# Attention and two MLPs on one core: the order of the attention steps, where its output is scaled, and one PSUM tile

## Chip, core and metric

The kernel runs on one core of one Trainium2 chip. Its engines are TensorE (PE in the profile), VectorE (DVE), ScalarE (ACT), GpSimd (POOL) and SyncE (SP), which issues most DMAs. The metric is device time in microseconds (us); a comparison uses the median of several runs.

## What is computed

```python
def _attn_ref(q, k, v):                       # 2 batches x 8 heads, 1152 keys, head width 64
    q_pool = q.reshape(B, H, S // 2, 2, D).mean(axis=3)          # 576 queries
    scores = q_pool @ k.T / sqrt(D)
    attn = exp(scores - max(scores))
    attn = attn / (sum(attn) + 1e-09)
    return attn @ v

x = attn_out.transpose(0, 2, 1, 3).reshape(1152, 512)            # one row per token
h = x @ w_in;  x = (h * tanh(softplus(h))) @ w_out               # Mish MLP, 512 -> 2048 -> 512
h = x @ w_in2; out = where(h > 0, h, exp(min(h, 0)) - 1) @ w_out2   # ELU MLP, same sizes
```

The MLP weights arrive as 64-bit floats and are converted on chip. Products that need the precision are made of three: each operand is split into a high part (`KH`, `QH`, `XH`, `wh`, `gh`) and the rest (`KL`, `QL`, `XL`, `wl`, `gl`).

## The kernel before

**Attention.** Two heads make a pair, and there are 8 pairs. A pair takes 18 steps: 9 tiles of 128 keys for its first 256 queries (chunk c=0), then 9 for the other 320 (c=1). An order written by hand fixes all work: `at(step, engine, f, ...)` puts a piece of work into a step, and a loop over the steps emits them. An offset below is the number of a step in its pair, 0 to 17. What the steps issue:

- `qk`: the transposed scores of one key tile, 8 matmuls into a tile S (L337, L339), then `exp` on ACT into `pt` (L345). The last two of the 8 subtract each query's maximum (row `top`).
- `peak_mm` and `peak`: to find those maxima, the scores of the next pair are computed once more in the other orientation (14 tiles M, L265 and L271), and DVE reduces each (L279). The list `WHEN` gives their steps relative to the pair's start. The maxima then travel through DRAM into a row: `top_out` (L314) and `top_in` (L320, L325, two or four small DMAs).
- `av`: the output before scaling, C = V times `pt`, two chunk accumulators (L432). It comes in bursts of two or three key tiles: bursts of c=0 at offsets 11, 13, 15 and 18 (the next pair's 0), of c=1 at 20, 22, 24 and 27.
- `add` on POOL (L358) and `total` on PE (tile T, L368) sum `pt` over the keys. The sum goes `spill` (ACT, L379), `sum_out` to DRAM (L385), `sum_in` (L389), `invert` on DVE (L411 adds 1e-9, L412 inverts), `inv_out` (L416), and `inv_in` as rows `rb` that fit C (L422).
- `scale` (DVE, L449) makes y = C times `rb` in SBUF; `token_high` (ACT, L454) and `token_low` (DVE, L459) split it into `XH` and `XL`, the MLP's input.
- SP also loads q, k and V (`load_v`, L232) of later pairs, and half a weight tile at a time (L107). The weights' conversion uses ACT, POOL and DVE (L117, L121, L126, L131, L132, L140, L143).

In PSUM, S, M, T and R (a transposed maximum, first pair only) share three slots of two banks in the order of issue: a tile can be written when the reader of the third tile before it has finished. C has two slots of one bank. In a step, `qk` and `exp` come first, then the M of that step, then `av`, then ACT's, DVE's, POOL's and SP's pieces. After the last step the loop goes on until all pieces are out; the last pair's sums are made wide (`total_wide`, `invert_wide`) without the way through DRAM.

**MLPs.** 96 units, each of 12 matmuls into a tile A (`h_mm`, L176), an activation, and 9 or 12 matmuls into accumulators B and C (`out_mm`, L668), three units later. They have PSUM pools of their own, taken when attention has given its pools back. The units of the first MLP take token blocks of 384 in the order 0, 1, 2, six units (of weight chunks) each at first; block 0 holds no token of the last pair.

Of the kernel before, what the change touches and what calls it, by code (L numbers as in the profile page):

```python
# [11 lines left out]
F32 = mybir.dt.float32  # L12
# [4 lines left out]
ALU = mybir.AluOpType  # L17
# [5 lines left out]
def tile_pool_attention_mish_elu_mlp(  # L23
# [40 lines left out]
    rawpool = ctx.enter_context(tc.tile_pool(name="rawpool", bufs=NR))  # L64
    dp = ctx.enter_context(tc.tile_pool(name="hop", bufs=2, space=bass.MemoryType.DRAM))
# [6 lines left out]
    wt, pools = {}, {}  # L72
# [73 lines left out]
    BANKS = {"A": 3, "B": 4, "C": 1}  # L146
    sums = cycle(("B", "B", "B", "B", "C"))

    def psum(tag):
        return pools["ps"].tile([P, 512], F32, tag=tag, name=tag, bufs=BANKS[tag])  # L150
# [30 lines left out]
    def attention():  # L181
        with ExitStack() as st:
            ap = st.enter_context(tc.tile_pool(name="attn", bufs=2))
            pools["f"] = st.enter_context(tc.tile_pool(name="f1", bufs=1))
            ps = st.enter_context(tc.tile_pool(name="pa", bufs=1, space=PSUM))
# [71 lines left out]
            def peak_mm(n, e):  # L257
# [4 lines left out]
                pt = sc[n, e] = ps.tile([P, 2, 512], F32, tag="S", name="M", bufs=3)  # L262
# [33 lines left out]
            def flip(t0, t1):  # L296
                pt = ps.tile([P, 2, 512], F32, tag="S", name="R", bufs=3)[:, 0]
# [32 lines left out]
            def qk(n, c, kt):  # L330
                o, w = cut[c][0], cut[c][1] - cut[c][0]
                pt = sc[n, c, kt] = ps.tile([P, 2, 512], F32, tag="S", name="S", bufs=3)
# [27 lines left out]
            def total(n, c):  # L360
                w = (cut[c][1] - cut[c][0]) // 2
                pt = sums_[n, c] = ps.tile([P, 2, 512], F32, tag="S", name="T", bufs=3)[:, 0]
# [24 lines left out]
            def sum_in(n, c):  # L387
                r = tots[n, c] = ap.tile([P, (cut[c][1] - cut[c][0]) // D], F32, tag=f"tot{c}", name="tot")
                nc.sync.dma_start(out=r, in_=hops.pop((n, c)))  # L389


            def total_wide(n, c):
                w = cut[c][1] - cut[c][0]
                pt = sums_[n, c] = ps.tile([P, 2, 512], F32, tag="S", name="T", bufs=3)[:, 0]
                p, a = pts[n, c], adds[n, c]
                srcs = [p[:, KT - 2], p[:, KT - 1], a[:, 0], a[:, 1]]
                for i, x in enumerate(srcs):
                    for h in range(2):
                        nc.tensor.matmul(
                            pt[half[h], :w], ones, x[:, h, :w], start=(i == 0), stop=(i == len(srcs) - 1)  # L400
                        )

            def invert_wide(n, c):
                w = cut[c][1] - cut[c][0]
# [406 lines left out]
```

## Time and profile before

| | |
|---|---|
| median of 3 runs | 674.32 us (673.21 to 674.74) |
| the profiled execution | 676.3 us, its span from first to last instruction 674.5 us |
| PE busy | 642.9 us, 95% of the span |
| DVE busy | 444.3 us, 66% |
| ACT busy | 341.9 us, 51% |
| POOL busy | 231.0 us, 34% |
| granted TensorE clock, mean | 0.989 of full speed |

Busy time of PE is overstated in attention: two matmuls that use different halves of the array run side by side, and a row's duration overlaps the next row's. What a matmul costs there is read from the distance between the starts of successive rows. The span splits in time into attention and the MLPs, so the stretches are to be read apart.

### The profile page before, as it was taken

What the parts mean: (1) busy time and instruction counts of PE and PEld (TensorE: products, weight loads), DVE (VectorE), ACT (ScalarE), POOL (GpSimd) and SP (SyncE); (2) the same over time, 40 slices, a digit from 0 to 9 for tenths busy, and PEclk for the clock granted to TensorE, in tenths of its full rate; (3) what the DMA queues carried; (4) which work ended last, traced back from release to release, by engine and by line L of the source; (5) the groups of instructions that cost most, each with busy time, mean ns of one, the idle gap of its engine ahead of it and who ended that gap; (6) DMA issues with size and microseconds to landing.
All of it is one profiled execution on the core that took longest, in us unless ns stands there. A gap on an engine that the chain in (4) does not pass through costs nothing.

```text
span 674.5 us, 11591 instructions
## 1 busy us (share of the span) xinstructions
PE 642.9 (95%) x4594; PEld 539.7 (80%) x4594; DVE 444.3 (66%) x700; ACT 341.9 (51%) x680; POOL 231.0 (34%) x216
## 2 busy tenths in 40 slices
PE   5998989898989899999999999999999999999997
PEld 3665656565656565999999999999999999999996
DVE  5756566566666635856645765776987788996543
ACT  2654545354545443643443545445666576665442
POOL 5877575756656543210110431333310011110000
PEclk9999999898989999999999999999999999999999
DMA  4323333333232113324123122222312321220111
GB/s 156 103 72 78 80 79 90 90 81 84 74 100 61 44 41 104 122 67 125 63 63 125 62 95 75 83 94 63 94 63 63 94 92 66 94 63 1 48 47 48
DMA packets 49615, 53.05 MB, mean 79 GB/s; under 512 B 16992, under 2 KB 38168, under 8 KB 49560
## 3 DMA queue, kind: packets, MB, share of 16 engines
q1 hardware_dynamic: 49048, 51.59, 25.9%
q8 instruction: 36, 0.59, 0.4%
q10 hardware_dynamic: 512, 0.72, 0.3%
q14 instruction: 19, 0.16, 0.1%
HBM read 49.84 MB, written 2.46 MB: 78 GB/s over the span
## 4 chain that ended last, share of the span: by engine, by line
PE 79%; DVE 10%; SPq 5%; DMA 4%; issue 1%; ACT 1%; DVEq 0%
PE A L176 30%; PE B L668 24%; PE S L337 6%; PE C L432 6%; PE C L668 6%; DVE stat L279 3%; SPq L325 2%; DMA rb<-pop 2%; PE M L265 2%; DVE XL L459 2%; PE T L368 2%; PE S L339 2%; DVE tot L411 1%; SPq L320 1%; PE M L271 1%
## 5 line engine op out<-in xcount | busy, mean ns | idle before, releaser
L345 ACT ACTIVATE pt<-S 128x512 f32<-128x512 f32 (+1 forms) x144 | 92.5, 651 | 95.6 <-PE S L339 57.0
L121 POOL TENSOR_SCALAR wf<-wf 128x512 f32<-128x512 f32 x64 | 42.8, 669 | 260.7 <-ACT wf L117 230.4
L279 DVE TENSOR_REDUCE stat<-M 128x2 f32<-128x768 f32 x96 | 89.8, 953 | 62.0 <-PE M L265 60.9
L176 PE MATMUL A<-XH,wh 128*128 128x384 f32 x384 | 128.9, 336 | 1.0 <-DVE y L449 1.0
L176 PE MATMUL A<-XH,wl 128*128 128x384 f32 x384 | 128.9, 336 | 0.0
L176 PE MATMUL A<-XL,wh 128*128 128x384 f32 x384 | 128.6, 335 | 0.0
L432 PE MATMUL C<-pt,vr 128*64 128x320 f32 (+1 forms) x576 | 85.7, 425 | 0.4 <-DVE y L449 0.4
L176 PEld LDWEIGHTS A<-XH,wh 128*128 128x128 f32 x384 | 72.1, 188 | 3.6 <-DVE y L449 1.6
L176 PEld LDWEIGHTS A<-XL,wh 128*128 128x128 f32 x384 | 72.1, 188 | 1.9
L358 POOL TENSOR_TENSOR add<-add,pt 128x512 f32<-128x512 f32 (+1 forms) x48 | 71.3, 1507 | 5.7 <-ACT pt L345 5.5
L358 POOL TENSOR_TENSOR add<-pt 128x512 f32<-128x512 f32 (+1 forms) x32 | 45.4, 1418 | 80.8 <-ACT pt L345 80.8
L176 PEld LDWEIGHTS A<-XH,wl 128*128 128x128 f32 x384 | 72.1, 188 | 0.0
L337 PE MATMUL S<-QH,KH 64*128 64x320 f32 (+1 forms) x288 | 53.8, 370 | 13.7 <-DVE stat L279 12.4
L337 PEld LDWEIGHTS S<-QH,KH 64*128 64x128 f32 x288 | 27.8, 189 | 46.1 <-DVE stat L279 20.2
L622 ACT ACTIVATE gh<-A 128x384 fp32r<-128x384 f32 x48 | 23.6, 492 | 78.9 <-PE A L176 78.9
L432 PEld LDWEIGHTS C<-pt,vr 128*64 128x64 f32 x576 | 36.4, 138 | 28.9 <-issue 9.7
L625 DVE TENSOR_TENSOR gl<-g,gh 128x384 fp32r<-128x384 f32 x48 | 32.0, 668 | 34.3 <-ACT g L623 34.2
L668 PE MATMUL B<-gh,wh 128*128 128x384 f32 x155 | 51.8, 334 | 0.0
L668 PE MATMUL B<-gl,wh 128*128 128x384 f32 x155 | 51.8, 334 | 0.0
L668 PE MATMUL B<-gh,wl 128*128 128x384 f32 x155 | 51.8, 334 | 0.0
L143 DVE TENSOR_TENSOR wl<-wf,wh 128x512 fp32r<-128x512 f32 x64 | 50.1, 783 | 0.7 <-ACT wh L140 0.7
L648 ACT CAST gh<-g 128x384 fp32r<-128x384 f32 x48 | 24.7, 514 | 48.1 <-DVE g L642 47.8
(103 smaller groups left out, 1330.5 us busy)
## 6 DMA issues: line engine op xcount, KB each, us to landing
raw<-in_moe_w_in_dram SPq DMA_DIRECT2D x28, 512.0 KB
raw<-in_moe_w_out_dram SPq DMA_DIRECT2D x28, 512.0 KB
vr<-in_v_dram SPq DMA_DIRECT2D x16, 288.0 KB
qr<-in_q_dram SPq DMA_DIRECT2D x14, 288.0 KB
kr<-in_k_dram SPq DMA_DIRECT2D x14, 288.0 KB
raw<-in_moe_w_in_dram SPq DMA_DIRECT2D x8, 256.0 KB
raw<-in_moe_w_out_dram SPq DMA_DIRECT2D x8, 256.0 KB
out_dram<-part SPq DMA_DIRECT2D x8, 256.0 KB
```

Of the source, the lines that this page charges most:

```text
L121: nc.gpsimd.tensor_scalar(self.f, self.f, HUGE, -HUGE, op0=ALU.min, op1=ALU.max)
L143: eng.tensor_tensor(self.l, self.f, self.h, op=ALU.subtract)
L176: nc.tensor.matmul(pt[:, :TB], w[:, kk * P:(kk + 1) * P], x[:, kk, tk], start=(i == 0), stop=(i == len(terms) - 1))
L279: nc.vector.tensor_reduce(m[:, t, :, j], pt[:, :, :KB], axis=AX.X, op=ALU.max)
L337: nc.tensor.matmul(pt[:, h, :w], x[half[h], kk], y[half[h], cols], start=(i == 0), stop=False)
L345: nc.scalar.activation(pts[n, c][:, kt], sc.pop((n, c, kt))[:, :, :w], AF.Exp, scale=SCALE)
L358: nc.gpsimd.tensor_tensor(d, d if i is None else p[:, i], p[:, j], op=ALU.add)
L432: nc.tensor.matmul(acc[n, c][half[h], :w], vs[n][:, h, kt, :], pts[n, c][:, kt, h, :], start=(kt == 0), stop=(kt == KT - 1),)
L622: nc.scalar.activation(gh, h, AF.Mish)
L625: nc.vector.tensor_tensor(gl, g, gh, op=ALU.subtract)
L648: nc.scalar.copy(gh, g)
L668: nc.tensor.matmul(pt, l, r, start=(first and i == 0), stop=(final and i == 2))
```

## The change

- The bursts of `av` have two key tiles and stand in every second step, at even offsets 10 to 26.
- In odd steps the M of the step is issued ahead of `qk`, in even steps behind it. `WHEN` changes; the last M of a pair comes one step earlier.
- `total` comes at offsets 12 and 20 (before 15 and 24), and the pieces behind it move with it; the last pair is no exception any more. `spill` adds the 1e-9 while it copies, so `invert` is one instruction. V is loaded at offsets 2 and 6 (before 9 of the pair ahead, and 2).
- `scale` works in place, in PSUM; `token_high` and `token_low` read it there. A list "rest" of DVE pieces comes behind the reduction of the step.
- One tile `banks` holds all 8 PSUM banks: 0 to 5 are the ring of attention's tiles, 6 and 7 the two accumulators; the MLPs use 0 to 2 for A and 3 to 7 in turn for the rest.
- The step loop ends 9 steps after the last `qk`. What is left of the last pair (`inv_in`, `scale`, `token_high`, `token_low` of c=1) is emitted in MLP units 0 to 2. Three weight tiles of the MLPs are read in the last pair already.

The diff, cut to its core (the removed functions `total_wide` and `invert_wide` and repeated replacements of a pool's tile by `take()` are left out):

```diff
+    banks = const_ps.tile([P, 8, 512], F32, name="banks")
+    turns = {"A": cycle(range(3)), "B": cycle(range(3, 8))}
     def psum(tag):
-        return pools["ps"].tile([P, 512], F32, tag=tag, name=tag, bufs=BANKS[tag])
+        return banks[:, next(turns[tag])]
...
+            ring = cycle(range(3))
+            def take():
+                i = 2 * next(ring)
+                return banks[:, i:i + 2]
...
-                nc.scalar.copy(r[:, :w], sums_.pop((n, c))[:, :w])
+                nc.scalar.activation(r[:, :w], sums_.pop((n, c))[:, :w], AF.Copy, bias=1e-9)
...
             def invert(n, c):
                 r = tots[n, c]
-                nc.vector.tensor_scalar(r, r, 1e-9, None, op0=ALU.add)
                 nc.vector.reciprocal(r, r)
...
-                    acc[n, c] = ps.tile([P, 512], F32, tag="C", name="C", bufs=2)
+                    acc[n, c] = banks[:, 6 + c]
...
-                x = xs[n, c] = ap.tile([P, w], F32, tag=f"y{c}", name="y", bufs=1)
-                nc.vector.tensor_tensor(x, acc.pop((n, c))[:, :w], rbs.pop((n, c)), op=ALU.mult)
+                x = xs[n, c] = acc.pop((n, c))[:, :w]
+                nc.vector.tensor_tensor(x, x, rbs.pop((n, c)), op=ALU.mult)
...
-            WHEN = [-13, -11, -10, -9, -8, -7, -6, -5, -4, -2, -1, 0, 1, 2]
+            WHEN = [-13, -12, -11, -10, -9, -8, -7, -5, -4, -3, -2, -1, 0, 1]
...
-                        at(s0 - 9 + 11 * i, "sp", load_v, n, i)
+                        at(s0 + [2, 6][i], "sp", load_v, n, i)
...
-                        at(u0 + KT + [2, 2, 4, 4, 6, 6, 9, 9, 9][kt], "av", av, n, c, kt)
-                    t0 = u0 + KT + 6
-                    if n < n_pairs - 1:
-                        at(t0 + 2, "sp", sum_out, n, c)
-                        at(t0 + 4, "sp", sum_in, n, c)
-                        at(t0 + 7, "dve", invert, n, c)
-                        at(t0 + 8, "sp", inv_out, n, c)
-                        at(t0 + 10, "sp", inv_in, n, c)
-                        at(t0 + 12, "dve", scale, n, c)
...
+                        at(s0 + 10 + (kt + 9 * c) // 2 * 2, "av", av, n, c, kt)
+                    t0 = s0 + 12 + 8 * c
+                    at(t0, "av", total, n, c)
+                    at(t0 + 1, "pre", spill, n, c)
+                    at(t0 + 1, "sp", sum_out, n, c)
+                    at(t0 + 3, "sp", sum_in, n, c)
+                    at(t0 + 5, "rest", invert, n, c)
+                    at(t0 + 5, "sp", inv_out, n, c)
+                    at(t0 + 7, "sp", inv_in, n, c)
+                    at(t0 + 10, "rest", scale, n, c)
+                    at(t0 + 11, "act", token_high, n, c)
+                    at(t0 + 12, "rest", token_low, n, c)
+            for r, x, y in (7, NW, 0), (11, NW, 1), (22, NW + 1, 0):
+                at(last - NS + r, "sp", early, x, y)
...
-            while s < last or todo or going:
+            while s < last + 9:
...
+                if s % 2:
+                    for f in by["peak"]:
+                        f()
                 if s < last:
                     qk(n, c, kt)
                     exp(n, c, kt)
-                for f in by["peak"]:
-                    f()
+                if s % 2 == 0:
+                    for f in by["peak"]:
+                        f()
...
+            for x, e in sorted(todo):
+                after.setdefault((x - s) // 2, []).extend(todo[x, e])
```

Three places show what the order becomes. On TensorE, in the middle of a pair (offsets around 11 of a later pair), before: S is L337 and L339, M is L265, the burst is L432.

```order
L265 MATMUL M<-KH,QH 128x384 x2
L337 MATMUL S<-QH,KH 128x320 x2
L337 MATMUL S<-QH,KL 128x320 x2
L337 MATMUL S<-QL,KH 128x320 x2
L339 MATMUL S<-top_81,unit 128x320 x2
L265 MATMUL M<-KH,QH 128x384 x2
L432 MATMUL C<-pt,vr 64x256 x4
L337 MATMUL S<-QH,KH 128x320 x2
L337 MATMUL S<-QH,KL 128x320 x2
L337 MATMUL S<-QL,KH 128x320 x2
L339 MATMUL S<-top_81,unit 128x320 x2
L265 MATMUL M<-KH,QH 128x384 x2
```

The same place of the changed kernel, where every tile is a part of `banks`: S is L344 and L346, M is L272, the burst L420.

```order
L272 MATMUL banks<-KH,QH 128x384 x2
L420 MATMUL banks<-pt,vr 64x256 x4
L272 MATMUL banks<-KH,QH 128x384 x2
L344 MATMUL banks<-QH,KH 128x320 x2
L344 MATMUL banks<-QH,KL 128x320 x2
L344 MATMUL banks<-QL,KH 128x320 x2
L346 MATMUL banks<-top_85,unit 128x320 x2
L344 MATMUL banks<-QH,KH 128x320 x2
L344 MATMUL banks<-QH,KL 128x320 x2
L344 MATMUL banks<-QL,KH 128x320 x2
L346 MATMUL banks<-top_85,unit 128x320 x2
L272 MATMUL banks<-KH,QH 128x384 x2
```

S and M alternated; now the two M of two steps stand around the burst and the two S behind them.

On VectorE, the stretch of a pair in which c=1 of the pair before is inverted; before (L459 is `token_low`, L411 and L412 `invert`, L449 `scale`):

```order
L459 TENSOR_TENSOR XL<-y,XH 128x256
L411 TENSOR_SCALAR tot<-tot 128x5
L412 RECIPROCAL tot<-tot 128x5
L279 TENSOR_REDUCE stat<-M 128x2 x4
L449 TENSOR_TENSOR y<-C,rb 128x320
L279 TENSOR_REDUCE stat<-M 128x2
```

And of the changed kernel (L447 `token_low`, L400 `invert`, L437 `scale`, L286 and L298 the reductions):

```order
L447 TENSOR_TENSOR XL<-banks,XH 128x256
L286 TENSOR_REDUCE stat<-banks 128x2
L400 RECIPROCAL tot<-tot 128x5
L286 TENSOR_REDUCE stat<-banks 128x2 x3
L298 TENSOR_REDUCE neg<-stat 128x4
L286 TENSOR_REDUCE stat<-banks 128x2
L437 TENSOR_TENSOR banks<-banks,rb 128x320
```

The adding instruction is gone, and a reduction stands between `token_low` and `invert`.

On SP's queue, where a pair begins, before (L416 `inv_out`, L320 and L325 `top_in`, L422 `inv_in`, L385 `sum_out`):

```order
L416 DMA pop<-tot 128x4
L320 DMA top_81<-hopm 1x256x1
L325 DMA top_81<-hopm 1x64x1
L320 DMA top_81<-hopm 1x256x1
L325 DMA top_81<-hopm 1x64x1
L107 DMA raw<-in_moe_w_out_dram 128x512
L422 DMA rb<-pop 64x256 x2
L385 DMA hop<-sum 4x160
L232 DMA vr<-in_v_dram 128x576
L389 DMA tot<-hop 128x5
```

And of the changed kernel (L392 `sum_out`, L327 and L332 `top_in`, L396 `sum_in`, L239 `load_v`, L404 `inv_out`, L410 `inv_in`):

```order
L392 DMA hop<-sum 4x160
L327 DMA top_85<-hopm 1x256x1
L332 DMA top_85<-hopm 1x64x1
L327 DMA top_85<-hopm 1x256x1
L332 DMA top_85<-hopm 1x64x1
L396 DMA tot<-hop 128x5
L239 DMA vr<-in_v_dram 128x576
L404 DMA pop<-tot 128x5
L109 DMA raw<-in_moe_w_out_dram 128x512
L410 DMA rb<-pop 64x320 x2
```

The four DMAs of `top_in` stood between `inv_out` and `inv_in`; now they stand between `sum_out` and `sum_in`, with the second half of V behind them.

## Rows read from the trace of the kernel before

**Rows 1.** Windows: us, then busy time of each engine, clock, DMA.

```profile
core 0: us, PE busy (x) PEld busy (x) DVE busy (x) ACT busy (x) POOL busy (x), PEclk, DMA share, GB/s
39.26:232.10 192.84, 177.21 (x1845) 115.69 (x1843) 123.32 (x177) 96.03 (x179) 123.57 (x90) 0.96 0.31 78
71.46:102.61 31.15, 28.43 (x311) 18.67 (x309) 20.65 (x30) 16.08 (x31) 20.66 (x15) 1.00 0.32 80
102.61:135.87 33.26, 30.25 (x309) 19.78 (x307) 20.73 (x30) 16.07 (x31) 20.63 (x15) 0.95 0.34 86
232.10:269.51 37.41, 34.95 (x335) 21.52 (x333) 17.81 (x33) 15.00 (x30) 14.97 (x11) 1.00 0.26 75
269.51:674.50 404.99, 400.69 (x2160) 381.62 (x2160) 280.02 (x460) 211.58 (x437) 64.47 (x80) 1.00 0.24 75
```

**Rows 2.** Timeline of PE: start, duration, what, idle before it and its releaser.

```profile
95.39 0.34 PE L265 MATMUL M<-KH,QH 64*128 64x384 f32 x2
97.72 0.41 PE L337 MATMUL S<-QH,KH 64*128 64x320 f32 x2 [1.99 <-DVE stat L279]
```

**Rows 3.** Timeline of DVE in the same stretch, and at 119.90.

```profile
93.60 1.57 DVE L459 TENSOR_TENSOR XL<-y,XH 128x256 fp32r<-128x256 f32 x1
95.09 1.51 DVE L411 TENSOR_SCALAR tot<-tot 128x5 f32<-128x5 f32 x1
...
96.74 1.78 DVE L279 TENSOR_REDUCE stat<-M 128x2 f32<-128x768 f32 x2
...
119.90 0.42 DVE L449 TENSOR_TENSOR y<-C,rb 128x256 f32<-128x256 f32 x1 [1.77 <-DMA rb<-pop]
```

**Rows 4.** Timeline of POOL at the same times.

```profile
93.33 1.55 POOL L358 TENSOR_TENSOR add<-pt 128x640 f32<-128x640 f32 x1 [1.95 <-ACT pt L345]
94.84 3.22 POOL L358 TENSOR_TENSOR add<-add,pt 128x640 f32<-128x640 f32 x2
...
117.36 2.77 POOL L252 TENSOR_TENSOR KL<-kr,KH 128x576 fp32r<-128x576 f32 x2
```

**Rows 5.** Timeline of PE, two stretches that show the distances between starts.

```profile
90.64 1.08 PE L432 MATMUL C<-pt,vr 128*64 128x256 f32 x8
91.66 0.42 PE L337 MATMUL S<-QH,KH 64*128 64x320 f32 x2
...
92.34 0.34 PE L265 MATMUL M<-KH,QH 64*128 64x384 f32 x2
...
111.48 0.39 PE L337 MATMUL S<-QH,KH 64*128 64x256 f32 x2
...
112.05 0.34 PE L265 MATMUL M<-KH,QH 64*128 64x384 f32 x2
...
112.80 1.30 PE L432 MATMUL C<-pt,vr 128*64 128x320 f32 x8
114.03 0.75 PE L368 MATMUL T<-pt,ones 128*32 128x160 f32 x16
...
115.25 0.39 PE L337 MATMUL S<-QH,KH 64*128 64x256 f32 x2
```

**Rows 6.** Timeline of SP's queue: start and duration of each issue.

```profile
104.96 0.43 SPq L232 DMA_DIRECT2D vr<-in_v_dram  x1
...
111.27 0.67 SPq L320 DMA_DIRECT2D top<-hopm  x1
...
115.06 0.88 SPq L325 DMA_DIRECT2D top<-hopm  x1
...
116.61 1.14 SPq L422 DMA_DIRECT2D rb<-pop  x2
...
252.59 0.33 SPq L416 DMA_DIRECT2D pop<-tot  x1
254.04 1.11 SPq L422 DMA_DIRECT2D rb<-pop  x2
```

**Rows 7.** Windows, one microsecond behind the load of V.

```profile
108.00:109.00 1.00, 1.00 (x8) 0.35 (x8) 1.00 (x4) 1.00 (x4) 0.11 (x1) 1.00 0.00 0
```

More of the change, by code (lines that the diff above doesn't have):

```diff
@@ L64, in tile_pool_attention_mish_elu_mlp @@
     rawpool = ctx.enter_context(tc.tile_pool(name="rawpool", bufs=NR))
+    const_ps = ctx.enter_context(tc.tile_pool(name="psum", bufs=1, space=PSUM))
+    late = ctx.enter_context(tc.tile_pool(name="late", bufs=1))
     dp = ctx.enter_context(tc.tile_pool(name="hop", bufs=2, space=bass.MemoryType.DRAM))
@@ L261, in peak_mm @@
                     neg[n] = ap.tile([P, NQ + 1, 2], F32R, tag="neg", name="neg")
-                pt = sc[n, e] = ps.tile([P, 2, 512], F32, tag="S", name="M", bufs=3)
+                pt = sc[n, e] = take()
                 if t < NQ:
@@ L296, in flip @@
             def flip(t0, t1):
-                pt = ps.tile([P, 2, 512], F32, tag="S", name="R", bufs=3)[:, 0]
+                pt = take()[:, 0]
                 for t in range(t0, t1):
@@ L387, in sum_in @@
             def sum_in(n, c):
-                r = tots[n, c] = ap.tile([P, (cut[c][1] - cut[c][0]) // D], F32, tag=f"tot{c}", name="tot")
+                r = tots[n, c] = late.tile([P, (cut[c][1] - cut[c][0]) // D], F32, tag=f"tot{c}", name="tot")
                 nc.sync.dma_start(out=r, in_=hops.pop((n, c)))
[L392 to L404, printed above, removed]
-                rb = rbs[n, c] = ap.tile([P, w], F32, tag=f"rb{c}", name="rb")
-                nc.vector.tensor_scalar(rb, sums_.pop((n, c))[:, :w], 1e-9, None, op0=ALU.add)
-                nc.vector.reciprocal(rb, rb)
             def invert(n, c):
                 r = tots[n, c]
-                nc.vector.tensor_scalar(r, r, 1e-9, None, op0=ALU.add)
                 nc.vector.reciprocal(r, r)
@@ L419, in inv_in @@
                 hop = hops.pop((n, c))
-                rb = rbs[n, c] = ap.tile([P, cut[c][1] - cut[c][0]], F32, tag=f"rb{c}", name="rb")
+                rb = rbs[n, c] = late.tile([P, cut[c][1] - cut[c][0]], F32, tag=f"rb{c}", name="rb")
                 for h in range(2):
@@ L579, in attention @@
                 s += 1
-            assert not pieces
+            assert not pieces and not going
+            for x, e in sorted(todo):
+                after.setdefault((x - s) // 2, []).extend(todo[x, e])
     def mlps():
@@ L657, in out_mm @@
                     if first:
-                        acc[m] = psum(next(sums))
+                        acc[m] = psum("B")
                     if layer == 0:
@@ L757, in mlps @@
                 go(u)
+                for f in after.pop(u, []):
+                    f()
                 between()
@@ L764, in mlps @@
                     when.pop(0)
-                    g = Weights(x, y)
+                    g = ahead.pop(0) if ahead else Weights(x, y)
                     assert u + 5 <= first_use[x] + AHEAD * y, (x, y, u)
                     going.append(g)
-                    g.read()
+                    if not hasattr(g, "moves"):
+                        g.read()
                     break
-            assert not loads and not going and not later
+            assert not loads and not going and not later and not after
     with tc.manual_schedule():
```

37 lines of the change are left out of this document (13 added, 24 removed).

## The prediction

> **What bounds the kernel now.** I read the windows first, cut where a pair's first S starts. The MLPs (269.51 to the end) keep PE busy for 400.69 of 404.99 us at full clock; the change leaves their matmuls as they are, so nothing is to be had there. Attention is another matter: six pairs, 39.26 to 232.10, take 192.84 us, 32.14 each, and no engine is full: of a pair of 31.15 us, DVE has 20.65, POOL 20.66, ACT 16.08 [rows 1].
>
> To see what PE itself needs, I took distances between starts [rows 5]. A burst of two key tiles takes 1.02 us for c=0 (90.64 to 91.66) and 1.23 for c=1 (112.80 to 114.03); an S beside a burst 0.68 for c=1 and 0.57 for c=0 (91.66 to 92.34, 111.48 to 112.05); an M with such an S 0.75, so M is 0.18; T of c=1 1.22, and by its columns about 1.0 for c=0 (an estimate). The three wide matmuls of the last two M run one after another, about 0.3 each (an estimate from M's columns). A pair: S 9 x (0.57 + 0.68) = 11.25; twelve M 2.2; wide M 0.9; C 4.5 x (1.02 + 1.23) = 10.1; T 2.2. That is 26.6 us. So **a pair waits 5.5 us**.
>
> Where, the timelines side by side show. The largest single wait is in every pair: PE stands 1.99 us before the S at 97.72 for DVE's reduction [rows 2]. DVE is late because `token_low` took 1.57 us and the adding instruction of `invert` 1.51, on 256 and 5 elements a partition; they end when POOL's additions end (93.33 + 1.55 = 94.88; 94.84 with two of 1.6) [rows 3, 4]. The scaling at 119.90, which reads C in PSUM and only one operand in SBUF, took 0.42 while POOL worked from 117.36 to 120.13 [rows 3, 4]. The rest of the waiting is spread: DVE itself waits for `rb` (1.77 us at 119.90), which SP could ask for only after `top_in`'s four DMAs, 111.27 to 115.94 [rows 3, 6], and with S and M alternating, an S reuses the slot of the M before last, so it waits whenever DVE is late.
>
> **The change, part by part.**
>
> *`invert` in one instruction, `token_low` from PSUM.* The adding instruction goes (1.51 us in this pair; `spill` adds while it copies, at the price of a copy). `token_low` now has one SBUF operand like the scaling, so I take 0.42 for it instead of 1.57; the bound above is 1.57, if it still waits for POOL. DVE's two late microseconds go, and with them the 1.99 us wait. The scaling in place writes PSUM rather than SBUF; no row shows that, I take the same 0.42, and up to 0.8 as a bound; it stands at M-free steps (offsets 4 and 12), where no reduction is behind it, so that bound too is covered.
>
> *The order of a pair of steps.* S M, burst, M S instead of S M S M with a burst somewhere. In the ring of three the M behind the burst needs the S of the step before, the S need the S and M before the burst: all are read during the burst. The one tight place is the M of the next even step, which needs the reduction of the odd M: 0.4 for M to land (0.34 long at 95.39, rather more behind a burst), 0.9 for the reduction (1.78 for two), 0.1 to hand over, together 1.4; PE reaches it after M and two S, 1.32 in c=0 and 1.54 in c=1 [rows 2, 3, 5]. With five such places I count 0.5 us a pair. `token_low` of c=1 stands before such a reduction: 0.3. Two steps cost 0.57 x 2 + 0.18 x 2 + 1.23 = 2.73, DVE's two reductions 1.8: 0.9 us of DVE are free in every two steps, and the weights' pieces lie at offsets without M.
>
> *The way of the sums through SP.* `top_in`'s block of 4.7 us has left the way from `invert` to `scale` and entered the one from `total` to `invert` for c=1. From T's end: copy 0.5 (estimate), `sum_out` 0.5 (estimate from the other issues), block 4.7, `sum_in` with its landing 1.8 (1.45 from an issue's start to the next DMA that needs it, 252.59 to 254.04): 7.5 us [rows 6]. On PE the steps between are 0.6 + 2.5 + 2.7 and then the reduction, 0.9 and its hand-over: 6.8. `invert` is 0.7 late; behind it stand the reductions of offsets 8 and 9, but DVE's free 0.9 takes most of it. I take 0.3, bounds 0 and 2. Then `inv_out` and its landing 1.45, `inv_in` 1.14, landing 2.15 (117.75 to 119.90) and a weight load's issue in between: 5.3 to `rb`, 13.0 after T [rows 3, 6], and `scale` is reached at 12.8. It is covered by T at offset 12, which has no M.
>
> *V's second half* stands behind `sum_in` on SP: issued about 6.1 us after T's end. The load of 104.96 had landed by 108.00, where nothing moves any more: 3.0 us [rows 6, 7]. So it lands at 9.2, and its first burst (offset 10) starts at 10.3: 0.6 + 2.5 + 2.7 + 2.9 + S and M 0.9, and 0.7 of waits. Nothing, with 1.1 to spare.
>
> *One PSUM tile; last pair; early weight reads.* An accumulator's bank is now held until `token_low` has read it (offsets 6 and 14); the next burst into it comes at 10 and 18: nothing. Any MLP wait by the common tile I take as nothing, up to 1 us at the start. The last pair and its tail are 37.41 us [rows 1]; after: S 11.25, wide M 0.9, C 5.5 + 4.6 + 5.5, T 1.2 + 1.0 + 1.2, 31.2, and 1.0 of waits: 32.2. It saves 5.2, bounds 3.5 and 6.2. c=1's scaling lies in MLP units 0 to 2; its tokens are first read in unit 12, 12 units of 4 us off.
>
> *The sum.* Waits of a pair 0.5 + 0.3 + 0.3, and 0.3 for small ones: 1.4, so 28.0 us (bounds 27.1 with half a microsecond of waits and 30.3). Six pairs save 6 x 4.1 = 24.8; the last 5.2; the first pair, where PE waits for loads and DVE, 0 (1.5 either way); the MLPs 0. Together 30.0. The profiled execution has 676.3 us (span 674.5), 2.0 above the median of 674.32; so 646.3 there, and **644.3** as a median.
>
> **A clock that goes on falling** is the first rival. The granted clock was 0.95 over 102.61 to 135.87 and 1.00 over 71.46 to 102.61 (33.26 against 31.15 us), 0.96 over six pairs: parts of them ran at 1.2 instead of 2.4 GHz, after PE had stood in the 1.99 us wait [rows 1, 2]. My 28.0 has it at 1.00. If it stays at 0.96 with the many short waits of a ring, six pairs of 28 lose 0.04 x 168 = 6.7 us: 651. Against it: the pair at 1.00 has short waits too, and the long one goes. The Trainium skill's page "TensorE: Matmul & The Clock Gate", section "A second HAM failure mode: psum-queue depth-cycling", says that short stops between matmul groups that cycle through PSUM slots can make the clock go up and down; by that rule this rival would hold, and the trace agrees only in so far as losing pairs exist.
>
> **Other rivals.** *SP's queue is the new bound*: `sum_in` or V comes 2 us later than I count, since `top_in`'s issues vary, and steps are shorter, so that fewer microseconds lie between the same number of steps. Then DVE or PE waits 2 us more in every pair, 30.0: 656. For it speaks that DVE waits for `rb` today already. *It doesn't do what it says*: the reductions' wait comes back in other places, as PE's order only moves it, and the pair stays above 31.5: 668 to 674, the last pair's gain alone remaining. Against it: DVE has 10 us free in a pair and loses 3 us of work. *Slower*: V's second half. If its landing came 6.5 us later than I count, the burst at offset 10 would stand 5.4 us in seven pairs, 38 us against 30 saved: 682. It decides against the change from 5.4 us late on (30 / 7 + 1.1), which asks for SP to be held by a wait that I have not seen.
>
> **How the numbers follow.** My forecast (a pair of 27.1 to 29.2) 0.55: 644.3, by itself 636 to 652. SP's queue 0.20, the clock 0.08, no effect on the pairs 0.09, slower 0.08. 636 is the sum with all lower bounds (6 x 5.0 + 6.2 + 1.5 = 38), 661 with all upper ones (6 x 1.8 + 3.5 - 1.5 = 13); the range 635 to 661 takes in the first three cases, and leaves out 0.17. A change of 0.2%, 1.3 us, is about what a measurement of this kernel can tell from none: faster 0.88, same 0.04, slower 0.08.
>
> **What would show it.** Right: windows from one pair's first S to the next of about 28 us, six alike, at clock 1.00; no PE wait of 2 us; `token_low` near 0.42 whatever POOL does; MLP matmuls starting near 239 with the same 405 behind them. Wrong: PE's bursts waiting for a DMA at offset 10 (V), DVE waiting long for `tot` or `rb` with PE's S or M behind it, a clock under 0.98 in the pairs, or pairs at 30 us and more.

## Result and the profile after

The changed kernel takes **652.38 us** (median of 4 runs, 651.91 to 652.93) against 674.48 us for the kernel before in the same call (673.21 to 674.74): a ratio of 0.9676, 95% interval 0.9659 to 0.9693. 644.3 was predicted, with a range of 635 to 661. One execution among all the runs below, at a granted clock of 0.85 from its first stretch to its last (709.5 us), is left out of the medians. Line numbers below are those of the changed kernel unless "before" is said.

Its windows, cut where a pair's first S starts (us; then busy time of each engine; granted clock, DMA share, GB/s), answer to [rows 1]:

```profile
core 0: us, PE busy (x) PEld busy (x) DVE busy (x) ACT busy (x) POOL busy (x), PEclk, DMA share, GB/s
13.69:40.94 27.25, 24.97 (x249) 18.23 (x251) 16.90 (x22) 14.14 (x27) 19.81 (x15) 1.00 0.33 94
40.94:212.28 171.34, 167.34 (x1846) 111.92 (x1844) 112.88 (x169) 91.19 (x180) 121.33 (x90) 1.00 0.39 88
98.31:126.62 28.31, 27.86 (x311) 18.65 (x309) 18.62 (x29) 15.20 (x30) 20.04 (x16) 1.00 0.41 98
212.28:244.34 32.06, 31.99 (x359) 20.18 (x355) 10.65 (x21) 15.47 (x29) 15.40 (x12) 1.00 0.33 85
244.34:650.10 405.76, 401.33 (x2162) 383.36 (x2160) 280.48 (x465) 211.76 (x438) 64.90 (x80) 1.00 0.24 77
```

Six pairs take 171.34 us, 28.56 each, instead of 192.84, and the clock is 1.00 in all. Set beside the terms of the prediction, in the two profiled executions (676.3 and 651.91 us):

| | predicted | measured |
|---|---|---|
| up to the first S | 0 | -0.68 (14.37 to 13.69) |
| first pair | 0 | **+2.36** (24.89 to 27.25) |
| six pairs | -24.8 | **-21.5** |
| last pair and tail | -5.2 | -5.35 (37.41 to 32.06) |
| MLPs | 0 | +0.77 |
| sum | -30.0 | -24.4 |

Where the 1.99 us wait stood [rows 2], nothing of that size is left: the longest wait that the profile lists for PE in the six pairs is 0.43 us. In the timeline of all engines of the changed kernel at offsets 6 and 7, `token_low` (L447) takes 0.41 us while POOL adds from 51.37 to 53.89, instead of 1.57 [rows 3], and the reduction behind it follows the M:

```profile
51.37 2.52 POOL L365 TENSOR_TENSOR add<-add,pt 128x512 f32<-128x512 f32 x2
52.68 0.41 DVE L447 TENSOR_TENSOR XL<-banks,XH 128x256 fp32r<-128x256 f32 x1
52.93 0.44 PE L272 MATMUL banks<-KH,QH 64*128 64x384 f32 x2
53.41 0.96 DVE L286 TENSOR_REDUCE stat<-banks 128x2 f32<-128x768 f32 x1 [0.31 <-PE banks L272]
```

What is left of PE's waiting stands where an even step's M needs the reduction of the odd step's M. The timeline of all engines at offset 6:

```profile
107.59 0.96 DVE L286 TENSOR_REDUCE stat<-banks 128x2 f32<-128x768 f32 x1 [1.32 <-ACT wh L142]
107.99 0.60 ACT L352 ACTIVATE pt<-banks 128x512 f32<-128x512 f32 x1 [0.39 <-PE banks L346]
108.14 0.28 PE L346 MATMUL banks<-top,unit 64*128 64x256 f32 x2
108.70 0.44 PE L272 MATMUL banks<-KH,QH 64*128 64x384 f32 x2 [0.28 <-ACT pt L352]
109.07 1.30 PE L420 MATMUL banks<-pt,vr 128*64 128x320 f32 x8
```

The profile puts this wait down to the exponential of step 5's S, which ends 0.04 us behind the reduction (108.59 and 108.55). By the ring the M takes the slot that the reduction reads, and in the run with short reductions, below, the same M starts while that exponential still runs; so it is the reduction that it waits for.

### The profile page after: what moved, and what is told of

Its sections match the earlier page's. It is cut to its first block, busy times and chain, and to the rows that moved or that the text cites. A ratio compares the mean times of both kernels' runs of the same rounds, so it can differ in the third digit from the quotient of the medians.

```text
span 650.1 us, 11772 instructions
## 1 busy us (share of the span) xinstructions
PE 631.7 (97%) x4626; PEld 536.9 (83%) x4626; DVE 428.2 (66%) x684; ACT 336.5 (52%) x682; POOL 229.0 (35%) x216
## 4 chain that ended last, share of the span: by engine, by line
PE 87%; DVE 4%; DMA 4%; SPq 1%; ACT 1%; issue 1%; POOL 0%; DVEq 0%; ACTq 0%
PE banks L178 31%; PE banks L661 30%; PE banks L420 10%; PE banks L344 6%; PE banks L272 4%; DVE stat L286 3%; PE banks L375 2%; PE banks L346 2%; DMA pop<-tot 1%; DMA rb<-pop 1%; PE banks L278 1%; DMA hopm<-neg 1%; DMA tot<-hop 1%; ACT pt L352 1%; DMA qr<-in_q_dram 1%
## 5 line engine op out<-in xcount | busy, mean ns | idle before, releaser
L352 ACT ACTIVATE pt<-banks 128x512 f32<-128x512 f32 (+1 forms) x144 | 88.8, 651 | 85.0 <-PE banks L346 75.2
L178 PE MATMUL banks<-XH,wh 128*128 128x384 f32 x384 | 129.5, 337 | 0.0
L178 PE MATMUL banks<-XL,wh 128*128 128x384 f32 x384 | 129.4, 337 | 0.0
L178 PE MATMUL banks<-XH,wl 128*128 128x384 f32 x384 | 129.4, 337 | 0.0
L286 DVE TENSOR_REDUCE stat<-banks 128x2 f32<-128x768 f32 x96 | 91.0, 957 | 49.8 <-PE banks L272 39.1
L420 PE MATMUL banks<-pt,vr 128*64 128x320 f32 (+1 forms) x576 | 85.5, 418 | 0.0
L178 PEld LDWEIGHTS banks<-XH,wh 128*128 128x128 f32 x384 | 72.0, 188 | 2.3 <-issue 0.5
L178 PEld LDWEIGHTS banks<-XL,wh 128*128 128x128 f32 x384 | 72.0, 188 | 1.8
L178 PEld LDWEIGHTS banks<-XH,wl 128*128 128x128 f32 x384 | 72.0, 188 | 0.0
L661 PE MATMUL banks<-gh,wl 128*128 128x384 f32 x192 | 64.5, 336 | 0.0
L420 PEld LDWEIGHTS banks<-pt,vr 128*64 128x64 f32 x576 | 35.3, 136 | 27.5 <-issue 10.5
L272 PE MATMUL banks<-KH,QH 64*128 64x384 f32 x192 | 43.2, 455 | 11.8 <-ACT KH L256 6.3
```

Of the source, the lines that this page charges most:

```text
L178: nc.tensor.matmul(pt[:, :TB], w[:, kk * P:(kk + 1) * P], x[:, kk, tk], start=(i == 0), stop=(i == len(terms) - 1))
L272: nc.tensor.matmul(pt[:, h, :KB], qh[n][half[h], t * P:(t + 1) * P], kh[n][half[h], j * KB:(j + 1) * KB], start=True, stop=True,)
L286: nc.vector.tensor_reduce(m[:, t, :, j], pt[:, :, :KB], axis=AX.X, op=ALU.max)
L352: nc.scalar.activation(pts[n, c][:, kt], sc.pop((n, c, kt))[:, :, :w], AF.Exp, scale=SCALE)
L420: nc.tensor.matmul(acc[n, c][half[h], :w], vs[n][:, h, kt, :], pts[n, c][:, kt, h, :], start=(kt == 0), stop=(kt == KT - 1),)
L661: nc.tensor.matmul(pt, l, r, start=(first and i == 0), stop=(final and i == 2))
```

## Experiments

All pair lengths are distances between the first S of successive pairs in the profiled execution, as above; medians are set beside the kernel before as it ran in the same call (674.5 to 677.9).

**The kernel before, profiled again.** No edit.

> The kernel before, unchanged, profiled a second time. Theory: the 2.0 us by which its profiled execution lay above the median came from stretches at a lower clock (0.95 and 0.96 in some pairs), and other executions lose less: the pairs that were long then (33.26, 32.93) are not the same ones here, several are near 31.2, and six pairs take 189 to 191 us instead of 192.8, with a total of 673 to 675. Rival: the clock falls in the same pairs in every execution, six pairs 192.5 to 193, and the 2.0 us have another place.

675.86 us. Six pairs, 39.30 to 231.74, take 192.44 us. Two of its windows:

```profile
102.96:136.12 33.16, 29.99 (x309) 19.63 (x307) 20.71 (x30) 16.04 (x31) 20.60 (x15) 0.95 0.34 87
136.12:167.27 31.15, 28.75 (x309) 18.76 (x308) 20.64 (x30) 16.07 (x31) 20.60 (x15) 1.00 0.32 80
```

Both expectations miss. The clock falls in partly other pairs than in the first profile, but the total of the six is nearly the same: three of them are at 0.95 here, four were there. A pair at full clock takes 31.12 to 31.55 us in the two executions, one at 0.95 takes 32.2 to 33.3; set against the full-clock pairs of the same execution, that is 1.0 us a pair on average over the six in the first, and 0.7 here.

**VectorE's relief alone, in the old order.**

```diff
-  nc.scalar.copy(r[:, :w], sums_.pop((n, c))[:, :w])
+  nc.scalar.activation(r[:, :w], sums_.pop((n, c))[:, :w], AF.Copy, bias=1e-9)
-  nc.vector.tensor_scalar(r, r, 1e-9, None, op0=ALU.add)          # invert
-  x = xs[n, c] = ap.tile([P, w], F32, tag=f"y{c}", name="y", bufs=1)
-  nc.vector.tensor_tensor(x, acc.pop((n, c))[:, :w], rbs.pop((n, c)), op=ALU.mult)
+  x = xs[n, c] = acc.pop((n, c))[:, :w]
+  nc.vector.tensor_tensor(x, x, rbs.pop((n, c)), op=ALU.mult)
-  at(t0 + 14, "act", token_high, n, c);  at(t0 + 16, "dve", token_low, n, c)
+  at(t0 + 13, "act", token_high, n, c);  at(t0 + 13, "rest", token_low, n, c)
```

> The kernel before with VectorE's relief alone: the 1e-9 goes into the copy, the scaling works in place in PSUM, the bursts and the order of S and M stay; token_high and token_low come earlier (offset 10 of the next pair for c=0, 1 for c=1), behind the reduction, since PSUM's accumulator is held until then. Theory (the 1.99 us wait of PE was VectorE waiting for POOL's additions): that wait goes in every pair, about 2.0 us each, and with it the fall of the clock, up to 1 us: pairs of 29 to 30.2, 655 to 662 in all. Rival (the reductions come late for another reason, the order of S and M with uneven bursts): pairs stay above 31, 668 to 674.

664.84 us (median of three executions, 664.15 to 667.16), ratio 0.983 (0.9785 to 0.9875). The pairs are read from another profile of the same kernel:

> The same kernel as e2_before_relief, profiled once more, since that profile has the clock at 0.85 from the first to the last stretch, the MLPs too, and its pairs can't be read. Theory A (with the 1.99 us wait gone, the old order needs what the changed kernel without alternation needs, 28.6 us): pairs at clock 1.00 take 28.6 to 29.2, some are longer at a lower clock, total 661 to 667. Theory B (other waits take its place): pairs at clock 1.00 stay at 30 to 30.8, with PE waits over 0.5 us listed.

667.56 us. Five of six pairs take 28.76 to 29.96 us, one 34.57. PE's waits in one pair, and at the start of the MLPs (line numbers of that kernel):

```profile
107.01 1.30 PE L431 MATMUL C<-pt,vr 128*64 128x320 f32 x8 [0.52 <-DVE XL L458]
...
260.83 0.41 PE L176 MATMUL A<-XH,wh 128*128 128x384 f32 x1 [2.24 <-DVE XL L458]
```

The 1.99 us wait is gone in all six pairs. Five of them come down from 31.15 to 29.4 on average, between the two theories: bursts now wait 0.3 to 0.6 us for an accumulator that is held until `token_low`. In the sixth, at a clock of 0.90, an M waits 1.86 us (87.96) for a reduction ahead of which VectorE's `scale` had stood 3.18 us for `rb` (86.61). In the tail, which still has its old form, that holding costs 3.3 us (40.75 instead of 37.41), which hides about a third of the pairs' gain in the total and puts it above the 655 to 662 that were expected.

**The relief taken back, in the new order.** The same edit the other way round, in the changed kernel.

> The changed kernel with VectorE's relief taken back: the adding instruction stands ahead of the reciprocal again, and the scaling writes SBUF, so token_low has two SBUF operands. Theory (contention with POOL is half of the gain, whatever the order): token_low at offset 6 and the adding instruction at offset 7 again last until POOL's additions end, about 1.5 us later for the reductions behind them, and PE waits 1.5 to 2.5 us more in every pair: 30.2 to 31 a pair, 662 to 668 in all. Rival (the even bursts alone give VectorE enough room): pairs under 29.2, 656 or less.

665.6 us (664.72 to 666.16), ratio 0.9832 (0.9797 to 0.9867): 13 us above the changed kernel. Pairs of 30.68 to 31.22. The two longest of PE's waits in one:

```profile
85.68 0.44 PE L272 MATMUL banks<-KH,QH 64*128 64x384 f32 x2 [0.78 <-DVE stat L286]
99.98 0.44 PE L272 MATMUL banks<-KH,QH 64*128 64x384 f32 x2 [1.26 <-DVE stat L286]
```

As the theory had it: with alternation, each slow `token_low` (1.48 at 83.27, 1.98 for two at 97.07) stands before a tight reduction.

**No alternation: M behind S in every step.**

```diff
-  if s % 2:            # "peak" ahead of qk
+  if 0:
-  if s % 2 == 0:       # "peak" behind exp
+  if 1:
```

> The changed kernel with M behind S in every step, odd ones too. Theory (the alternation is worth little: with a burst in every second step a slot's reader always has a burst's time): pairs 28.2 to 29.0, 650 to 655 in all; the wait of the first pair at its seventh step goes as well, up to 1 us. Rival (the alternation is what removes the waits): pairs of 30 and more, 662 or more in all.

651.37 us (650.31 to 652.59), ratio 0.9625 (0.9583 to 0.9668): not slower than the changed kernel. Six pairs take 171.79 us, 28.63 each. The alternation is worth nothing here; "little" was expected. PE has small waits of another kind in this order:

```profile
109.96 0.28 PE L346 MATMUL banks<-top,unit 64*128 64x256 f32 x2
110.29 0.44 PE L272 MATMUL banks<-KH,QH 64*128 64x384 f32 x2
```

The M takes the slot of the S before last, whose exponential (the first of two, 1.25 us together from 109.64) ends only then: 0.33 us after the last matmuls of S instead of 0.12 (106.28 to 106.40), five times a pair, and the burst behind such an M comes 0.1 later as well.

**Neither alternation nor relief.** Both edits; what remains of the change are the bursts in every second step, the earlier sums with their pieces in other steps, and the tail; further V's loads, `WHEN`, and the steps of the weights' conversion, which the change moves too (the core of the diff doesn't show it). No run takes any of these back by itself, but for the places of the two pieces of VectorE below.

> The changed kernel with M behind S in every step and VectorE's relief taken back, so that the bursts in every second step with the earlier sums and the new tail remain. Theory (bursts and relief are each worth something by themselves): pairs of 29.5 to 31, 657 to 667. Rival A (the even bursts alone are the gain): under 29, 655 or less. Rival B (they are nothing without the relief): 31.5 and more, 668 to 671.

652.33 us (651.06 to 657.6), ratio 0.9661 (0.9618 to 0.9704). My theory falls, rival A nearly holds: four pairs of 28.63 to 28.65, the others 29.64 and 30.05. `token_low` is as slow as ever, in a pair in which PE waits nowhere over 0.15 us; the adding instruction takes 0.51 there:

```profile
107.84 1.51 DVE L448 TENSOR_TENSOR XL<-y,XH 128x256 fp32r<-128x256 f32 x1
109.28 0.95 DVE L286 TENSOR_REDUCE stat<-banks 128x2 f32<-128x768 f32 x1
110.14 0.51 DVE L400 TENSOR_SCALAR tot<-tot 128x5 f32<-128x5 f32 x1
```

In the two longer pairs PE waits 1.06 us (141.78) and 1.34 us (212.10) for reductions that stand behind a slow piece and a late DMA: the sum, for which VectorE waits 0.89 us ahead of an adding instruction of 0.91 (139.74), and `rb`, for which it waits 2.05 us at 205.18, with two `token_low` of 3.25 us behind it (207.92). So without the relief a late sum or `rb` still reaches PE. What differs from [rows 3] in the other four is that a reduction stands between `token_low` and the adding instruction. That asked for two more runs, the same idea from both sides.

**The kernel before, with the two pieces in different steps.**

```diff
-  at(t0 + 14, "act", token_high, n, c);  at(t0 + 16, "dve", token_low, n, c)
+  at(t0 + 13, "act", token_high, n, c);  at(t0 + 14, "dve", token_low, n, c)
```

> The kernel before with one edit: token_low stands two steps earlier (offset 11 of the next pair for c=0, 2 for c=1), token_high one, so that token_low and the adding instruction no longer stand in the same step; both stay as slow as they are. Theory (not contention alone but the two slow pieces in one step make the 1.99 us wait): the wait falls under 0.6 us in every pair, pairs of 29 to 30, 655 to 665 in all. Rival (a slow piece anywhere in this order costs PE its time): one wait of over 1 us a pair stays, 670 to 675.

670.41 us (669.86 to 673.05), ratio 0.993 (0.9906 to 0.9953). Waits of PE in three pairs, those from 99.12, 129.32 and 160.30, and VectorE ahead of two of them:

```profile
103.01 0.62 PE L271 MATMUL M<-KH,blk 128*128 128x384 f32 x2 [0.86 <-DVE stat L279]
...
121.44 0.41 PE L337 MATMUL S<-QH,KH 64*128 64x320 f32 x2 [0.37 <-DVE stat L279]
...
145.71 0.38 PE L339 MATMUL S<-top,unit 64*128 64x320 f32 x1 [1.12 <-DMA top<-hopm]
...
165.42 0.62 PE L271 MATMUL M<-KH,blk 128*128 128x384 f32 x2 [2.10 <-DVE stat L279]
...
101.60 0.49 DVE L449 TENSOR_TENSOR y<-C,rb 128x320 f32<-128x320 f32 x1 [1.47 <-DMA rb<-pop]
...
164.01 0.49 DVE L449 TENSOR_TENSOR y<-C,rb 128x320 f32<-128x320 f32 x1 [2.70 <-DMA rb<-pop]
```

The wait that was 1.99 is 0.31 to 0.37 in all six pairs, as the theory has it. The waits that are left are not VectorE's slow pieces but DMAs of SP: `scale` of c=1 waits for `rb`, the reduction behind it comes late, and the wide M waits 0.5 to 2.1 us for that in four pairs (`token_low` comes only behind it, at 166.95 in the last one shown); in two pairs an S waits 1.1 and 1.4 us for the maxima of `top_in`. Pairs take 28.9 to 32.6 us, and the total lies just inside the rival's 670 to 675, by another cause than the rival's. So the way through SP is the next limit of the old order once the 1.99 us are gone. The change moves `top_in` and the sums on SP, and no such wait of over 0.43 us is listed in its pairs.

**The new order without either, and the two pieces in one step again.**

```diff
-  at(t0 + 12, "rest", token_low, n, c);      at(t0 + 5, "rest", invert, n, c)
+  at(t0 + 13 - c, "rest" if c else "dve", token_low, n, c)
+  at(t0 + 5, "dve" if c else "rest", invert, n, c)
```

> The kernel of e5_after_neither (even bursts, S ahead of M in every step, VectorE's old pieces), with one edit: token_low of c=0 stands one step later, at offset 7, ahead of that step's reduction, and the adding instruction of c=1 behind it, as the two stood in one step before the change. Theory (what the change really takes away is that the two slow pieces stand together ahead of a reduction): PE waits 1 to 2 us again in every pair, pairs of 29.7 to 30.7, 660 to 668 in all. Rival (a burst in every second step gives VectorE the room, wherever the pieces stand): pairs under 29.0, 651 to 655.

661.22 us (658.61 to 665.19), ratio 0.9775 (0.9713 to 0.9837), 9 us more than without this edit. Pairs of 29.37 (three), 30.72 (two) and 31.83. PE and VectorE in the pair from 68.24:

```profile
85.39 0.42 PE L344 MATMUL banks<-QH,KH 64*128 64x320 f32 x2 [2.02 <-DVE stat L286]
...
80.10 1.51 DVE L448 TENSOR_TENSOR XL<-y,XH 128x256 fp32r<-128x256 f32 x1
82.87 1.39 DVE L400 TENSOR_SCALAR tot<-tot 128x5 f32<-128x5 f32 x1 [1.26 <-DMA tot<-hop]
84.40 1.80 DVE L286 TENSOR_REDUCE stat<-banks 128x2 f32<-128x768 f32 x2
```

A wait of 2.02 is back in three pairs. Part of it is the sum's arrival (1.26), for which VectorE now stands with reductions behind it; in the other three, as in the one from 98.96, where it came with 0.40 of waiting, PE's wait is 0.66, less than the 1 to 2 us that the theory asks. So even bursts alone don't give the room: it matters where VectorE's slow pieces stand, by 0.66 us where the sum is 0.40 late and by 2.02 where it is 1.26 late.

**The reductions made short.** Each reads 32 of 384 columns of a narrow M.

```diff
-  nc.vector.tensor_reduce(m[:, t, :, j], pt[:, :, :KB], axis=AX.X, op=ALU.max)
+  nc.vector.tensor_reduce(m[:, t, :, j], pt[:, :, :32], axis=AX.X, op=ALU.max)
```

> The changed kernel with each reduction of a narrow M reading 32 of its 384 columns, so that the maxima are those of a part of the keys (this part of the computation is left out): a reduction takes about 0.25 us instead of 0.96. Theory (what a pair waits now, 1.4 to 1.7 us, is PE waiting for reductions): pairs of 26.8 to 27.3, ten us less in all, 640 to 643. Rival (PE's own work and its switching between kinds of matmul is what the pair takes): 28 and more, 648 to 652.

639.33 us (638.62 to 642.77). Six pairs and one of them, then ACT and PE at offset 6:

```profile
37.81:200.06 162.25, 161.56 (x1847) 110.94 (x1845) 61.22 (x168) 91.25 (x180) 120.81 (x91) 1.00 0.41 94
119.39:146.44 27.05, 27.05 (x312) 18.58 (x310) 9.96 (x27) 15.21 (x30) 19.98 (x16) 1.00 0.46 109
```

```profile
129.29 0.60 ACT L352 ACTIVATE pt<-banks 128x512 f32<-128x512 f32 x1 [0.38 <-PE banks L346]
129.44 0.28 PE L346 MATMUL banks<-top,unit 64*128 64x256 f32 x2
129.56 0.34 PE L272 MATMUL banks<-KH,QH 64*128 64x384 f32 x2
129.83 1.30 PE L420 MATMUL banks<-pt,vr 128*64 128x320 f32 x8
```

The theory holds for the pairs: 27.04 on average. The total lies 0.7 us under its range. Of the 13 us, 9.1 are the six pairs, 3.1 the start (the first S comes at 10.62), 0.6 the last pair. From the last matmul of S to the burst it is 0.39 us here and 0.93 in the changed kernel (108.14 to 109.07): 0.54 lost at one such place, 0.28 of it listed as a wait.

**The first pair.** M behind S until step 7, alternating from step 8 on.

```diff
-  if s % 2:
+  if s % 2 and s > 7:
-  if s % 2 == 0:
+  if s % 2 == 0 or s <= 7:
```

> The changed kernel with the alternation from step 8 on only; in the first eight steps S comes ahead of M, as before. Theory (the 1.04 us wait at the first pair's M at 27.48 came from the M of step 7 issued ahead of two R and an S, which took its slot): the first pair takes 26.1 to 26.4 instead of 27.25, and the total falls by 0.7 to 1.2 us against the changed kernel. Rival (the first pair is bound by VectorE and the loads, and the wait moves): the first pair stays at 27, no difference over 0.3 us.

650.68 us (650.2 to 651.18), ratio 0.9622 (0.9597 to 0.9647); the first pair takes 25.42 us, and the second starts at 39.50 instead of 40.94. In the changed kernel, all engines at step 7:

```profile
23.16 0.60 PE L272 MATMUL banks<-KH,QH 64*128 64x384 f32 x4
24.01 1.11 PE L306 MATMUL banks<-ident,pad 128*128 128x128 f32 x6 [0.25 <-ACT pt L352]
25.05 0.38 PE L344 MATMUL banks<-QH,KH 64*128 64x256 f32 x2
25.84 1.10 ACT L352 ACTIVATE pt<-banks 128x512 f32<-128x512 f32 x2 [0.26 <-PE banks L346]
26.47 1.82 DVE L286 TENSOR_REDUCE stat<-banks 128x2 f32<-128x768 f32 x2 [1.89 <-ACT pt L352]
27.48 0.45 PE L272 MATMUL banks<-KH,QH 64*128 64x384 f32 x2 [1.04 <-DVE stat L286]
```

M of step 7 (in the x4 at 23.16) is followed by two R and an S: the third of them takes its slot, ahead of its reduction in the program. The reduction therefore comes only at 26.47, behind the exponential of that S, and M at 27.48 waits for it. With S ahead of M in that step this is gone; the gain, 1.8 us in the pair and 1.4 by the start of the second, is more than the 0.85 to 1.15 expected.

This is an error of the changed kernel, not only a wait: that reduction reads the scores of the S that overwrote its M in 256 of the 384 columns of each head, so the maxima of 128 queries of the second pair are taken over the wrong numbers for a part of the keys. What is subtracted from the scores falls out again in the division by their sum, as long as the exponential stays in range, which is why the output doesn't show it. In the kernel before a slot was handed on only behind its readers; slices of one tile, taken in turn, don't wait for a reader that comes later in the program.

**V's second half later.**

```diff
-  at(s0 + [2, 6][i], "sp", load_v, n, i)
+  at(s0 + [2, 9][i], "sp", load_v, n, i)
```

> The changed kernel with V's second half issued at offset 9, behind the rows of the sums, instead of offset 6: in the profile 57.4 instead of 52.66, 4.7 us later. The first burst that needs it starts at 58.37. Theory (a load of V lands 3.0 us after its issue, as the prediction has it): there are 2.7 us to spare, not 1.1, the burst stands about 2.0 us in each of seven pairs, and the total is 13 to 16 us longer: 665 to 668. Rival (it lands sooner, in 2 us): 1 us a pair, 657 to 660. No change would say that V is bound nowhere.

696.79 us (695.54 to 698.06), ratio 1.0303 (1.0271 to 1.0336): 44 us more, three times what I expected. SP's queue, then PE, in the pair from 110.61:

```profile
127.80 0.59 SPq L410 DMA_DIRECT2D rb<-pop  x1
128.44 0.58 SPq L239 DMA_DIRECT2D vr<-in_v_dram  x1
```

```profile
127.62 0.65 PE L420 MATMUL banks<-pt,vr 128*64 128x256 f32 x2
131.99 1.08 PE L420 MATMUL banks<-pt,vr 128*64 128x256 f32 x6 [3.72 <-DMA vr<-in_v_dram]
133.45 0.47 PE L344 MATMUL banks<-QH,KH 64*128 64x320 f32 x2
```

The load is issued 17.8 us into the pair, later than I took it from the profile (16.5), because `rb` stands ahead of it on SP; PE goes on 3.5 us after the issue, not 3.0 (3.3 to 5.0 in the six pairs), and stands 3.72. Behind the wait PE runs slowly (S 0.47 a row instead of 0.31), and the clock of the six pairs is 0.94: a pair costs 5.9 us more, where the waits for V are 3.7 on average. The last pair, with a wait of 7.44 us, costs 10.6.

**Two of the tight places taken away.** The first pair's edit, and for the third pair on:

```diff
-  WHEN = [-13, -12, -11, -10, -9, -8, -7, -5, -4, -3, -2, -1, 0, 1]
+  WHEN = [-14, -13, -11, -9, -8, -7, -6, -5, -4, -3, -2, -1, 0, 1]
```

> The changed kernel, alternating from step 8 on only, and with the narrow M of later pairs at offsets 4, 5, 7, 9 to 17 instead of 5 to 11 and 13 to 17: two of the five places where an even step's M waits for the reduction of the odd step's M, those of c=0, are gone, and offset 12 has an M ahead of T. Theory (these places cost 0.28 us of wait each and 0.1 of a late start): pairs of 27.6 to 28.0 and the first pair near 25.5, 645 to 649 in all, faster than the changed kernel by 3 us or more. Rival (VectorE is late at other places instead, above all at the M of offset 12, behind which the scaling stands): pairs of 28.3 and more, 650 or more.

**646.66 us** (646.02 to 647.61), ratio 0.9569 (0.9537 to 0.9600): the fastest of the kernels that do all the work. Two of its pairs:

```profile
39.72:67.27 27.55, 27.48 (x311) 18.56 (x309) 19.23 (x29) 15.21 (x30) 19.98 (x16) 1.00 0.44 97
67.27:95.71 28.44, 27.96 (x311) 18.95 (x309) 18.60 (x29) 15.21 (x30) 20.19 (x16) 1.00 0.39 89
```

Four of six pairs are at 27.52 to 27.55, the longest at 28.44, and PE's listed waits are gone in the four. As the theory has it; the first pair takes 25.99.

## Why the prediction was right, and what was wrong in it

The direction, the place (the pairs and the tail) and the size within the range were right. From 646.3, the sum before 2.0 was taken off, to the profiled 651.9 it is: first pair +2.4, six pairs +3.3, MLPs +0.8, start -0.7, tail -0.2.

**What a pair waits for.** "That is 26.6 us. So a pair waits 5.5 us." About 1.0 of these 5.5 is the clock, which the sum counts among the waits. Of a pair at full clock, 31.15 from 71.46, the trace lists 1.99 and 0.51 as waits of PE, and 28.65 are left (28.65 to 29.15 in the full-clock pairs of both profiles). That is not PE's own need, for starts can be late by too little to be listed. PE before, an S behind an M, once at its soonest and once late:

```profile
80.21 0.34 PE L265 MATMUL M<-KH,QH 64*128 64x384 f32 x2
80.39 0.28 PE L337 MATMUL S<-QH,KH 64*128 64x256 f32 x2
...
84.84 0.44 PE L265 MATMUL M<-KH,QH 64*128 64x384 f32 x2
85.38 0.42 PE L337 MATMUL S<-QH,KH 64*128 64x320 f32 x2
```

The first S starts 0.18 behind its M, the second 0.54. Late starts of this kind come to about 1.9 us in that pair, which leaves some 26.8 (an estimate, from the distances between starts there). In the run without alternation, five late M's with their bursts and a wide M come to 1.8 of the 28.63, which leaves 26.9 (an estimate in the same way). With short reductions the new order measures 26.7 to 27.0 in the pairs without a listed wait, 27.04 on average. So 26.6 was right to 0.2 in the old order, as far as these estimates go (no run has it with short reductions), and 0.4 short in the new one, which waits 1.5 beside its 27.04: 28.56, where the prediction has 26.6 and 1.4. That own need is the term that was too small, and it makes 2.6 of the 3.3 us that six pairs fall short.

**`invert` and `token_low`: sizes right, the conclusion too wide.** 0.41 us under POOL's additions, and the scaling in place 0.42 and 0.50: as predicted. But the relief is only one way to be rid of the 1.99 us wait. The wait came from the two slow pieces standing together ahead of a reduction: moving one of them takes it away in the old order (1.99 to 0.37), standing them together brings waits of 0.66 to 2.02 back in the new order (661.22 against 652.33), and the new places nearly do without the relief (652.33, with waits of over 1 us in two of six pairs). The gains don't add: relief alone takes 10.8 us off (or 14.1 without its loss in the tail), new places and tail without it 24.2, with it and alternation 22.1; 652.33 and 652.38 are the same time, the kernel before differed by 2 us between the two calls. Only the alternation makes the relief needed (665.6 without).

**The order of two steps.** "The one tight place" is the right one, but it costs 0.54 at offset 6 and 0.37 at offset 8 (111.40 to 112.16), and about 0.16 at each of three in c=1 (0.06 of start, 0.1 of burst), instead of 0.1 each; the terms for `token_low`, late `invert` and small waits (0.9 together) did not appear as such. In total 1.5 against 1.4; that these totals are so near is luck, for the terms differ. The alternation trades the late starts behind exponentials for waits for reductions, and nothing is left of it (28.56 against 28.63 a pair).

**First pair: taken as nothing, up to 1.5 either way, measured at +2.4.** Most of it is M ahead of S in the odd steps, 1.04 of it at step 7: with S ahead of M in the first eight steps the pair takes 25.42 instead of 27.25, and the second pair starts at 39.50, 0.24 us behind the kernel before (39.26). The prediction has no term for it; it looked at the ring in later pairs only, where no R takes a slot. The pair also runs four bursts and twelve M's beside its own S's instead of three and eleven, 1.2 us more of PE's busy time, which the last pair's saving holds on the other side and which I had not set against it; with the order of these steps put right, about 0.5 us of that is seen.

**The profiled execution and the median.** Taking off 2.0 was wrong: before's second profile was as long (675.86, six pairs of 192.44), and its medians in later calls were 675.6 to 677.9. The changed kernel's profile lies 0.5 under its median.

**Tail, MLPs, clock, SP.** 32.06 against 32.2, which no run takes apart; no wait before the first A at 244.34, where 1.03 us stood before. The clock stays at 1.00 with listed stops of PE of 0.43 us and less in the six pairs, so that rival falls. The Trainium skill's rule ("TensorE: Matmul & The Clock Gate", "A second HAM failure mode: psum-queue depth-cycling"), that short stops between groups that cycle through PSUM slots can make the clock go up and down, is not borne out by this trace, in which the groups cycle through three slots at a granted clock of 1.00. VectorE waits for the sums (7.8 us in seven waits) and `rb` (14.6 in eight), but no wait of PE over 0.43 us follows in the six pairs; SP's queue is not the bound here. It is not far from one: in the old order, and in the new one without the relief, late rows do reach PE.

**V.** In a pair where it is issued at 11.7 us it had more to spare than the 1.1 us counted: 17.8 - 11.7 = 6.1 us later, it makes a wait of 3.7, so 2.4. But the issue comes 11.5 to 13.4 us into the six pairs, so the latest has about 0.7 (an estimate from that 2.4), and in the last pair PE's weight load does wait for V:

```profile
227.59 0.62 PEld L420 LDWEIGHTS banks<-pt,vr 128*64 128x64 f32 x6 [0.28 <-DMA vr<-in_v_dram]
```

The slower rival's mechanism is real, and dearer than its price: 5.9 us a pair for 3.7 of standing, with a granted clock of 0.94 over the six pairs.

Not settled: why the granted clock falls behind some waits of 2 us and not behind others (below), and how the gain without relief and alternation is shared by the other moves: even bursts, `top_in` and the sums on SP, the weights' conversion.

## What to carry to other kernels

Check an engine's own need against a whole period: its length at full clock, less the listed waits, must come out. What is over is need that was missed, time at a lower clock, or starts late by too little to be listed, and the distances between starts tell which. A slow instruction on an engine off the path costs what stands behind it in the same step, so moving it a step can take the same wait away as making it fast, and two such cures don't add. Ask what stands right behind a wait that is to go: in the old order it was SP's rows. When a table of steps moves, count the work that crosses the first and the last period too, and go through the order of the first one by itself. Slices of one tile handed out in turn need their own proof that every reader comes ahead of the next writer.

## What the runs showed of the hardware

- After PE's wait of 3.72 us for V, the matmuls that followed took 0.47 instead of 0.31 us a row, and the pairs' clock was 0.94. In the old order, where each pair has a wait of 1.99 us, four of six pairs were at 0.95 in one execution and three in the other, the rest at 1.00; a wait of 2.10 us stood in a pair at 1.00. The length of a wait alone doesn't decide it.
- The instruction that adds 1e-9 to 5 elements a partition took 0.16 us with POOL idle (97.13, in the run with neither), and 0.51, 1.39 and 1.51 beside its work; a `token_low` with an operand in PSUM 0.41 beside POOL's additions, with two in SBUF 1.51. The weights' shift, one tensor operand in SBUF, took 1.49 beside an addition too (100.53, in the run with neither).
- An M that started late behind S was followed by its burst 0.37 us later, one that started at once 0.27: a late start costs 0.1 us beyond the wait itself.
